# GpSimd waits for the VectorE instruction ahead of it at their shared port: an attention and mixture-of-experts kernel with its order found anew

## The chip, the cores and the metric

The kernel runs on one core of a Trainium2 chip. The metric is the device time of one execution in microseconds. Before the change the median of three runs is 1009.34 us (1007.29 to 1016.77).

## The reference, cut to what matters

Eight batches of 12 heads, 448 tokens, head size 64. Queries and keys are normalised, attention is computed, and its output (3584 tokens of 768) goes through a mixture of experts in which each token uses the one expert of eight that its logits choose.

```python
q_n, k_n = rmsnorm(q, g_q), rmsnorm(k, g_k)
scores = q_n @ k_n.T / sqrt(64)
attn = exp(scores - max) / (sum + 1e-9)
x = (attn @ v) as [3584, 768]
e = argmax(x @ w_gate); gate = softmax(x @ w_gate)[e]
out = gate * sigmoid((x @ w_output_gate)[e]) * (relu(x @ w1[e]) @ w2[e])
```

## The kernel before, in words

The attention part works on 48 head pairs, numbered 0 to 47 (six to a batch). A pair's steps are small operations named `step.pair`, such as `vl.17`. `sq` and `ms` give the mean squares; `n` and `qg` normalise (L419, L424); `hi`, `hj` write the float16 half of queries and keys and `lo`, `lp` the rest (L436); two transposing DMAs `Th`, `Tl` turn them. `M0` to `M3` are score products, of which `x0` to `x3` take the row maxima on VectorE (L456); `NT`, `nt` (L469) turn these; `S0` to `S3` are the scores with the maxima taken off; `e` and `f` are the exponentials as float32 and float16, `p0` to `p3` their difference (L509, on GpSimd or VectorE); `vh`, `vl` split the values in the same way (L515, L519); `A0` to `A3`, `A6` multiply by the values. For the pairs that the string `WHOLE` marks, block 0 isn't split: `Aw` (L535) multiplies it in float32, 16 matrix products, in place of `f0`, `p0` and `A0`. `av1`, `av2`, `av` divide (L553, L556, L562), `tr`, `th`, `lg`, `la` give the router's logits.

After each batch a chain `r0` to `r7` of small VectorE steps picks experts and slots (`r6.e1` to `r6.first_expert` also the first two experts, L763 to L772), and four indirect DMAs `z0` to `z3` from GpSimd (L740) write the slot table. The expert stage then gathers tokens (`xg`, L1006, indirect DMA from GpSimd), splits them (`xh` on ScalarE, `xl` on VectorE, L1053), turns them by DMA (`xt`), splits the weights (`wh` on ScalarE, `wl` on VectorE, L982) and multiplies (`g1`, L1085 to L1087, and `g2`); `sc` scatters rows out (L1100). Only its first steps belong to the order below; the rest of it is in code order.

What order the engines' instructions have is written out by hand in tables: `ENGINES` gives each movable step two engines, `SECOND` picks one by pair, and `RANK` and `ONCE` give each step its place. `Order.run` sorts all steps by place, and the loop in `moe` issues them; each engine takes its own in that order, and waits only for its data and buffers. Each step also carries a mark, `port`, from this table, which nothing before the change reads:

```python
PORT = {
    DVE: ("hi", "hj", "n", "qg", "lo", "lp", "vh", "vl"),
    POOL: ("mh", "n", "qg", "lo", "lp", "p0", "p1", "p2", "p3"),
}
```

The steps `x`, `ms`, `av`, `p` on VectorE read PSUM or one tile and aren't in it; nor are `xl`, `wl` and the chain `r`.

Of the kernel before, what the change touches and what calls it, by code (L numbers as in the profile page):

```python
# [75 lines left out]
    "p0": "100000101110100011110011110001010111101100000110",  # L76
    "p1": "000000000001001001100001101001000000100000000101",
    "p2": "101010000000001011110001000100000000100101010000",
    "p3": "000001011000000100000000000001000001100000010000",
    "lo": "001011111100110100100100000010000000100000001011",  # L80
    "lp": "000011010000101000100100011011010110110101100010",
    "hi": "000000000000000000000000000000000000000000010001",
    "hj": "000000000010000000000000010000001000000010000000",
# [1392 lines left out]
```

## Time and profile before

| what | value |
|---|---|
| median of three runs | 1009.34 us |
| the profiled execution, its own time | 1007.91 us |
| its span, first to last instruction | 1006.1 us |
| mean granted clock of TensorE in it | 0.979 |
| busy in the span: TensorE, VectorE, ScalarE, GpSimd | 91%, 65%, 58%, 46% |

The span is cut by what the core does: attention from 0 to about 506 us, the expert stage from there. Shares over the whole span mix the two, so the rows below are by stretch. In the rows PE is TensorE, DVE VectorE, ACT ScalarE, POOL GpSimd; a name such as `vl<-vf,vh` is output and inputs with buffer numbers left out.

### The profile page before, as it was taken

The page shows a single profiled execution, that of the slowest core. Times are in us where ns is not written, and L with a number is a line of the kernel's source. Part 1 is how long each engine was busy: PE and PEld are TensorE (multiplying, and loading weights), DVE is VectorE, ACT ScalarE, POOL GpSimd, SP SyncE. Part 2 cuts the span into 40 slices and gives each one's busy share as a digit, 9 for nine tenths or more (in the row PEclk, how much of TensorE's full clock was granted, in tenths as well). Part 3 has the DMA queues.
Part 4 walks back from the last instruction along what each step waited for, and adds up shares of the span by engine and source line. Part 5 has one row for each costly group of instructions (what it writes and reads, how often), then busy time and mean ns, then how long its engine had stood idle before and what let it go on. Part 6 is the DMA issues. An engine that isn't in the chain of part 4 may idle for free. (4 is left out here: it accounts for less than half of the span.)

```text
span 1006.1 us, 28072 instructions
## 1 busy us (share of the span) xinstructions
PE 919.1 (91%) x12072; PEld 645.1 (64%) x12072; DVE 658.7 (65%) x1072; ACT 581.9 (58%) x913; POOL 466.0 (46%) x355
## 2 busy tenths in 40 slices
...
GB/s 228 164 177 159 124 208 132 156 114 192 134 163 119 198 169 134 94 108 105 174 237 161 151 262 251 189 108 160 179 119 238 73 209 202 113 225 207 74 2 46
DMA packets 182541, 157.36 MB, mean 156 GB/s; under 512 B 152449, under 2 KB 160263, under 8 KB 176269
## 3 DMA queue, kind: packets, MB, share of 16 engines
...
HBM read 96.73 MB, written 22.59 MB: 119 GB/s over the span
## 5 line engine op out<-in xcount | busy, mean ns | idle before, releaser
L509 POOL TENSOR_TENSOR pl<-p,ph 128x896 f16<-128x896 f32 (+1 forms) x111 | 181.6, 1646 | 54.6 <-PE psa L548 23.0
L456 DVE TENSOR_REDUCE Z<-psM 128x2 f16<-128x896 f32 (+1 forms) x192 | 180.8, 967 | 15.4 <-PE psM L451 11.3
L478 PE MATMUL pss<-ss 64*128 64x448 f16 (+1 forms) x1152 | 146.6, 359 | 10.3 <-DVE Z L456 3.7
L504 ACT ACTIVATE ph<-pss 128x896 f16<-128x896 f32 (+1 forms) x144 | 113.6, 797 | 36.4 <-PE pss L484 27.9
L1085 PE MATMUL g1e<-xTe,w0he 128*128 128x384 f16 x384 | 126.0, 328 | 9.0 <-DMA xTe<-x16e 5.4
L1100 POOL DMA_INDIRECT out<-oe,tie x24 | 25.6, 1068 | 230.4 <-DVE oe L1122 201.5
L1086 PE MATMUL g1e<-xTe,w0he 128*128 128x384 f16 x384 | 125.9, 328 | 0.0
L1087 PE MATMUL g1e<-xTe,w0le 128*128 128x384 f16 x384 | 125.8, 328 | 0.0
L548 PE MATMUL psa<-vh,ph 128*128 128x65 f16 (+1 forms) x1152 | 110.9, 198 | 2.7 <-issue 2.7
L545 PE MATMUL psa<-vl,ph 128*128 128x64 f16 (+1 forms) x1152 | 109.9, 194 | 1.8 <-issue 1.5
L548 PE MATMUL psa<-vh,pl 128*128 128x65 f16 (+1 forms) x1152 | 110.1, 196 | 1.3 <-issue 1.3
L548 PEld LDWEIGHTS <-ph 128*128 128x128 f16 (+1 forms) x1152 | 94.5, 102 | 11.9 <-issue 8.7
L496 ACT ACTIVATE p<-pss 128x896 f32<-128x896 f32 (+1 forms) x120 | 94.9, 798 | 12.2 <-PE pss L484 9.8
L545 PEld LDWEIGHTS <-ph 128*128 128x128 f16 (+1 forms) x1152 | 95.1, 103 | 2.6 <-issue 2.4
L548 PEld LDWEIGHTS <-pl 128*128 128x128 f16 (+1 forms) x1152 | 95.1, 101 | 1.1 <-issue 1.0
L451 PE MATMUL psM<-ss 64*128 64x448 f16 (+1 forms) x384 | 68.9, 375 | 27.2 <-DMA ss<-X 18.5
L1085 PEld LDWEIGHTS <-w0he 128*128 128x128 f16 x624 | 61.5, 99 | 37.2 <-issue 10.0
L484 PEld LDWEIGHTS <-sel 64*128 64x128 f16 (+1 forms) x1536 | 61.8, 99 | 35.5 <-issue 4.5
L478 PEld LDWEIGHTS <-ss 64*128 64x128 f16 (+1 forms) x1152 | 53.3, 98 | 47.7 <-issue 21.4
L1086 PEld LDWEIGHTS <-w0he 128*128 128x128 f16 x624 | 61.6, 99 | 28.6 <-issue 5.1
L1087 PEld LDWEIGHTS <-w0le 128*128 128x128 f16 x624 | 61.6, 99 | 28.3 <-issue 3.7
L982 DVE SCALAR_TENSOR_TENSOR w0le<-wste,w0he 128x1024 f16<-128x1024 f32 x48 | 59.8, 1255 | 27.2 <-ACT w0he L980 27.2
...
## 6 DMA issues: line engine op xcount, KB each, us to landing
...
ss<-X SPq DMA_TRANSPOSE x96
...
tab<-val,slot POOLq DMA_INDIRECT x32
xge<-xs,tie POOLq DMA_INDIRECT x24
```

The source lines that it names most:

```text
L451: T.matmul(o, lhsT=side(0, 0, h, c, n), rhs=side(0, 1, h, 0, S), start=True, stop=True)
L456: V.tensor_reduce(out=o, in_=m, op=ALU.max, axis=AX.X, negate=True)
L478: T.matmul(o[h], lhsT=side(wk, 1, h, 128 * u, n), rhs=side(wq, 0, h, 0, S), start=k == 0, stop=False)
L484: T.matmul(o[h][:, a : a + m], lhsT=self.sel[r, 3 * h + c, 0:n], rhs=st["nt"][r, q], start=False, stop=c == 3)
L496: A.activation(out=t, in_=st[f"S{u}"], func=AF.Exp)
L504: A.activation(out=st[f"ph{u}"], in_=st[f"S{u}"], func=AF.Exp)
L509: return (V if eng == DVE else Pl).tensor_tensor(out=st[f"pl{u}"], in0=st[f"e{u}"], in1=st[f"ph{u}"], op=ALU.subtract)
L545: T.matmul(out[:, 0:D], lhsT=st[f"ph{u}"][:, k, q], rhs=vl[:, jv, :], start=False, stop=False, skip_group_check=True)
L548: T.matmul(out, lhsT=p, rhs=vh[:, jv, :], start=u == j == w == 0, stop=u == 3 and w == 2, skip_group_check=True)
L1085: nc.tensor.matmul(o, lhsT=wh[:, sl], rhs=xT[:, 0, k, 0:n], start=k == 0, stop=False)
L1086: nc.tensor.matmul(o, lhsT=wh[:, sl], rhs=xT[:, 1, k, 0:n], start=False, stop=False)
L1087: nc.tensor.matmul(o, lhsT=wl[:, sl], rhs=xT[:, 0, k, 0:n], start=False, stop=k == KD - 1)
```

## The change

The loop that issues the steps remembers the last VectorE step that is marked `port`. A later GpSimd step that is marked, or that is an indirect DMA (it has a transfer time `xfer`), is made to wait for it; `follow` adds that dependency.

```diff
-WHOLE = "111111111010101010101110111100101010101010100110"
+WHOLE = "111111111010101010101110111100101010101010101111"
...
-                add("xh" + x, ACT, 800, [f"xg{m}.{c}"], lambda q=q, c=c: q["T"][c][0](), [("x16", ["xt" + x])])
-                add("xl" + x, DVE, 860, ["xh" + x], lambda q=q, c=c: q["T"][c][1]())
+                add("xh" + x, ACT, 800, [f"xg{m}.{c}"] + [f"o0.{2 * NCB - 1}"] * (m == 2), lambda q=q, c=c: q["T"][c][0](), [("x16", ["xt" + x])])
+                add("xl" + x, DVE, 860, ["xh" + x] + [f"o1.{2 * NCB - 1}"] * (m == 2), lambda q=q, c=c: q["T"][c][1]())
...
+        held = None
         for o in self.order.run():
-            o["fn"]()
+            ins = o["fn"]()
+            if o["eng"] == DVE and o["port"]:
+                held = ins
+            elif o["eng"] == POOL and None not in (held, ins) and (o["port"] or o["xfer"]):
+                self.follow(ins, [held], "port")
```

All of `SECOND`, `RANK` and `ONCE` is replaced. One line of each of two tables:

```diff
-    "th": "000000000100101010000001000001000000010110010011",
+    "th": "110000001010100000100011010100000001111011000011",
...
-k.edges 0 k.gd 5 k.blank 6 k.cst 7 s00.mean 13 s00.guess 14 s00.sm 17 s00.r 18 k.g 21 s01.mean 22 s01.guess 23 s01.sm 26 s01.r 27 k.flat 28 k.sel 34
+k.edges 0 k.cst 4 k.gd 5 s00.mean 12 s00.guess 13 s00.sm 16 s00.r 17 k.g 20 s01.mean 21 s01.guess 22 s01.sm 25 s01.r 28 k.sel 29 s02.mean 55
```

Pairs 44 and 47 become whole (two more `Aw`, two fewer `f0`, `p0`, `A0`). By step, the number that VectorE does goes from 12 to 18 of `th`, 8 to 13 of `p3`, 14 to 16 of `n`, 21 to 24 of `qg`, 2 to 5 of `vh`; and down from 11 to 9 of `p1`, 6 to 3 of `hi` and `hj` together, 37 to 36 of `lo` and `lp` together. Of `nt` VectorE does 12 where it did 17, ScalarE the rest.

What the waits look like, on GpSimd's queue around the table writes of batch 1 (`slot1`), first before the change. A name's first number is the pair, as in `qkt24` or `pl17_3` (`p3.17`); the bracket names the semaphores that an instruction waits for, those of VectorE as DVE.

```order
L740 DMA tab_85<-val_81,slot1_3580 30720x2
L436 TENSOR_TENSOR X1_119<-qkt22_2299,X1_119 128x8x64 [waits DMAHW6_49]
L419 TENSOR_TENSOR qkt26_3251<-qkt26_3251,y40_3482 128x896 [waits DMAHW4_49]
L509 TENSOR_TENSOR pl16_1_4231<-p3216_1_3831,ph16_1_3837 128x896
L740 DMA tab_85<-val_81,slot1_3580 30720x2
L424 TENSOR_TENSOR qkt24_2638<-qkt24_2638,g_74 128x448 [waits Pool_49]
L509 TENSOR_TENSOR pl17_3_4352<-p3217_3_4217,ph17_3_4254 128x448 [waits PE_49,Activation_49]
L436 TENSOR_TENSOR X1_119<-qkt22_2299,X1_119 128x8x64 [waits Activation_49]
```

And the same place of the changed kernel:

```order
L509 TENSOR_TENSOR pl18_3_4526<-p3218_3_4293,ph18_3_4287 128x448 [waits DVE_49,PE_49,Pool_49]
L740 DMA tab_85<-val_81,slot1_3609 30720x2 [waits DMASW2_49,DMASW3_49,DMASW1_49,DMASW0_49]
L424 TENSOR_TENSOR qkt29_3884<-qkt29_3884,g_74 128x448 [waits Pool_49]
L509 TENSOR_TENSOR pl18_1_4599<-p3218_1_4470,ph18_1_4462 128x896 [waits Activation_49]
L509 TENSOR_TENSOR pl19_1_4654<-p3219_1_4499,ph19_1_4523 128x896 [waits PE_49,Activation_49]
L740 DMA tab_85<-val_81,slot1_3609 30720x2
L740 DMA tab_85<-val_81,slot1_3609 30720x2 [waits DVE_49]
L740 DMA tab_85<-val_81,slot1_3609 30720x2
```

Before, no row of the eight names VectorE; now two do, and rows without the name follow a wait that already covers them. Over all of GpSimd's queue, of the rows of L419, L424, L436, L509, L740, L1006 and L1100, 73 name VectorE's semaphore before and 108 after.

The second place is the handover to the expert stage, GpSimd's queue from the table writes of batch 6 (`slot6`) to the gathers for the first expert (`xge0`). Before:

```order
L740 DMA tab_85<-val_81,slot6_10310 30720x2 x3
L509 TENSOR_TENSOR pl43_1_10535<-p3243_1_10302,ph43_1_10282 128x896 [waits Activation_49]
L509 TENSOR_TENSOR pf44_0_10396<-p3244_0_10407,pf44_0_10396 128x896 [waits Activation_49]
L509 TENSOR_TENSOR pl44_1_10671<-p3244_1_10507,ph44_1_10482 128x896 [waits PE_49,Activation_49]
L509 TENSOR_TENSOR pl44_2_10723<-p3244_2_10604,ph44_2_10583 128x896 [waits Activation_49]
L509 TENSOR_TENSOR pl44_3_10772<-p3244_3_10721,ph44_3_10700 128x448 [waits Activation_49]
L1006 DMA xge0_10767<-xs_84,tie0_10766 128x768 [waits DMAHW5_49,DMAHW6_49,DMAHW4_49,DMAHW7_49,DMAHW1_49,DMAHW0_49]
```

Now:

```order
L740 DMA tab_85<-val_81,slot6_10329 30720x2 x3
L509 TENSOR_TENSOR pl44_1_10691<-p3244_1_10567,ph44_1_10541 128x896 [waits PE_49,Activation_49]
L509 TENSOR_TENSOR pl44_3_10745<-p3244_3_10713,ph44_3_10742 128x448 [waits PE_49,Activation_49]
L509 TENSOR_TENSOR pl45_3_10781<-p3245_3_10689,ph45_3_10693 128x448 [waits PE_49,Pool_49]
L509 TENSOR_TENSOR pl45_1_10804<-p3245_1_10783,ph45_1_10762 128x896 [waits DVE_49,Activation_49]
L509 TENSOR_TENSOR pl45_2_10890<-p3245_2_10855,ph45_2_10797 128x896 [waits DVE_49,Activation_49]
L1006 DMA xge0_10858<-xs_84,tie0_10857 128x768 [waits DMAHW5_49,DMAHW4_49,DMAHW6_49,DMAHW3_49,DMAHW7_49,DMAHW1_49,DMAHW0_49]
```

Three of the four long differences that stood behind the table writes are gone from there (`p1.43`, `p0.44` and `p2.44`; `p0.44` no longer exists), and others with waits on VectorE stand in their place.

## Rows read from the trace of the kernel before

**Rows 1.** Busy time by stretch: stretch, length, then each engine's busy us and instructions

```profile
0.00:50.00 50.00, 24.64 (x266) 13.83 (x268) 42.78 (x59) 37.88 (x71) 36.28 (x44) 0.93 0.75 197
50.00:350.00 300.00, 282.75 (x5229) 209.90 (x5225) 283.01 (x496) 266.24 (x448) 243.35 (x169) 1.00 0.71 155
350.00:450.00 100.00, 95.11 (x1856) 70.92 (x1857) 84.08 (x162) 77.70 (x127) 82.56 (x58) 1.00 0.53 131
450.00:515.00 65.00, 52.63 (x917) 39.39 (x914) 44.57 (x76) 37.04 (x54) 35.87 (x25) 0.89 0.62 153
515.00:1006.00 491.00, 463.97 (x3813) 311.03 (x3811) 204.30 (x283) 163.01 (x216) 67.96 (x62) 0.98 0.54 159
```

**Rows 2.** TensorE's waits, 50 to 515 us: for whom, total us, times, longest

```profile
PE g1e L1085 <- DMA xTe<-x16e: 5.4, 1, 5.4
...
PE pss L478 <- DVE pl L509: 3.2, 2, 2.9
...
PE psa L548 <- DVE xr L562: 2.5, 2, 2.1
```

**Rows 3.** Groups by line and shape, VectorE, 0 to 505 us: busy, mean ns

```profile
L436 DVE TENSOR_TENSOR X<-qkt,X 128x512 f16<-128x512 f32 x37 | 29.3, 804 | 0.7 <-POOL pl L509 0.5
...
L509 DVE TENSOR_TENSOR pl<-pss,ph 128x896 f16<-128x896 f32 x25 | 27.0, 1085 | 5.8 <-issue 2.7 <-ACT pss L493 1.6 <-POOL X L436 1.1
L519 DVE SCALAR_TENSOR_TENSOR vl<-vf,vh 128x384 f16<-128x384 f32 x30 | 20.9, 698 | 0.1
L519 DVE SCALAR_TENSOR_TENSOR vl<-vf,vh 128x512 f16<-128x512 f32 x18 | 17.2, 957 | 0.0
L419 DVE TENSOR_TENSOR qkt<-qkt,y 128x896 f32<-128x896 f32 x14 | 15.1, 1091 | 0.0
L424 DVE TENSOR_TENSOR qkt<-qkt,g 128x448 f32<-128x448 f32 x21 | 14.4, 688 | 0.1
...
L397 DVE COPY xT<-pstr 128x448 f32<-128x448 f32 x10 | 6.1, 607 | 0.1
...
L509 DVE TENSOR_TENSOR pl<-pss,ph 128x448 f16<-128x448 f32 x8 | 4.9, 615 | 0.4 <-PE psa L548 0.4
L469 DVE TENSOR_SCALAR nt<-psNT 128x128 f16<-128x128 f32 x17 | 4.8, 281 | 0.4 <-PE psNT L461 0.4
```

**Rows 4.** Timeline, 199.5 to 206.9 us, GpSimd and then VectorE: start us, us

```profile
200.00 0.97 POOL L740 DMA_INDIRECT tab<-val,slot  x1 [0.17 <-issue]
200.99 1.15 POOL L424 TENSOR_TENSOR qkt<-qkt,g 128x448 f32<-128x448 f32 x1
202.08 1.04 POOL L509 TENSOR_TENSOR pl<-p,ph 128x448 f16<-128x448 f32 x1
203.07 1.16 POOL L436 TENSOR_TENSOR X<-qkt,X 128x512 f16<-128x512 f32 x1
...
200.60 4.18 DVE L519 SCALAR_TENSOR_TENSOR vl<-vf,vh 128x512 f16<-128x512 f32 x1
```

**Rows 5.** Timeline, 460 to 468 us, GpSimd and then VectorE

```profile
460.63 1.90 POOL L509 TENSOR_TENSOR pl<-p,ph 128x896 f16<-128x896 f32 x1
...
464.32 1.88 POOL L509 TENSOR_TENSOR pl<-p,ph 128x896 f16<-128x896 f32 x1
...
461.00 5.23 DVE L764 SCALAR_TENSOR_TENSOR most<-score,top,cst 128x8 f32<-128x8 f32 x1
...
466.34 0.15 DVE L770 SCALAR_TENSOR_TENSOR score<-most,score 128x8 f32<-128x8 f32 x1
```

**Rows 6.** Timeline, 485 to 508 us, VectorE and then TensorE

```profile
485.54 1.04 DVE L1053 TENSOR_TENSOR x16e<-xge,x16e 128x768 f16<-128x768 f32 x1 [2.20 <-ACT x16e L1050]
...
490.35 0.51 DVE L519 SCALAR_TENSOR_TENSOR vl<-vf,vh 128x384 f16<-128x384 f32 x1
490.78 2.64 DVE L1053 TENSOR_TENSOR x16e<-xge,x16e 128x768 f16<-128x768 f32 x1
...
501.25 0.67 DVE L519 SCALAR_TENSOR_TENSOR vl<-vf,vh 128x512 f16<-128x512 f32 x1
...
485.08 1.82 PE L535 MATMUL psa<-vf,pf 128*128 128x65 f32 x16
```

More of the change, by code (lines that the diff above doesn't have):

```diff
@@ L75 @@
 SECOND = {
[L76 to L83, printed above, removed]
@@ new lines @@
+    "p3": "001001000101001000010010001000100000110100000001",
+    "lo": "000011011000101011000011100110100100001010000011",
+    "lp": "000001101011000011100011001010111000010010000000",
+    "hi": "100000000000000000000000000000000000000000000000",
+    "hj": "000000000000000000000000000000000010000000000001",
+    "vh": "000000000000000000000000000000010000001000000111",
+    "th": "110000001010100000100011010100000001111011000011",
+    "n": "000001101010100110100010000110010000100011000010",
@@ L151 @@
-k.ltri 548 k.tab 588 r0.first 613 r0.mx 617 r0.eq 618 r0.ex 619 r0.eqe 620 r0.em 622 r0.oh 627 r0.zz 628 r0.rank 638 k.xs 639 st.0 641 r0.z 644
-r0.count 645 r0.exps 646 r0.pos 649 r0.sum 650 r0.pr 656 r0.sum1 657 r0.slot 661 r0.den 662 s31.mean 684 s31.guess 686 s31.sm 690 s31.r 694 r0.val 756
-s40.mean 864 r0.z0 869 s40.guess 870 s40.sm 876 s40.r 878 r0.z2 890 r0.z1 896 r1.first 899 r1.mx 901 r1.eq 902 r1.eqe 905 r1.ex 906 r0.z3 907
-r1.em 908 r1.oh 911 r1.zz 912 r1.rank 915 r1.z 918 r1.count 920 r1.exps 921 r1.pos 929 r1.sum 930 r1.pr 931 r1.sum1 933 r1.slot 934 r1.den 935
@@ L155 @@
-r1.val 974 st.1 976 r1.z0 978 r1.z1 986 r1.z2 1021 r1.z3 1053 s41.mean 1062 s41.guess 1063 s41.sm 1070 s41.r 1072 s50.mean 1185 s50.guess 1186
-s50.sm 1193 s50.r 1198 st.2 1234 r2.first 1237 r2.mx 1239 r2.eq 1240 r2.eqe 1245 r2.ex 1246 r2.em 1248 r2.oh 1251 r2.zz 1254 r2.z 1257 r2.exps 1279
-r2.rank 1294 r2.count 1302 r2.pos 1307 r2.sum 1308 r2.pr 1316 r2.sum1 1318 r2.slot 1319 r2.den 1325 r2.val 1326 s51.mean 1346 s51.guess 1348
-r2.z0 1349 s51.sm 1352 s51.r 1354 r2.z1 1377 r2.z3 1390 r2.z2 1400 s60.mean 1548 s60.guess 1549 s60.sm 1556 s60.r 1557 r3.first 1623 r3.mx 1628
@@ L159 @@
-r3.eq 1629 r3.eqe 1631 r3.em 1632 r3.ex 1634 r3.oh 1637 r3.zz 1645 r3.z 1647 r3.rank 1658 r3.count 1664 r3.exps 1669 r3.sum 1671 r3.sum1 1673
-r3.pos 1674 r3.den 1675 s61.mean 1685 s61.guess 1687 r3.pr 1692 s61.sm 1694 s61.r 1695 r3.slot 1698 r3.val 1716 r3.z0 1736 r3.z1 1742 r3.z2 1770
-st.3 1822 r3.z3 1828 s70.mean 1867 s70.guess 1870 s70.sm 1875 s70.r 1876 r4.first 1904 r4.mx 1906 r4.eq 1911 r4.ex 1913 r4.eqe 1915 r4.em 1917
-r4.oh 1918 r4.zz 1919 r4.rank 1942 st.4 1946 r4.z 1947 r4.exps 1950 r4.count 1955 r4.sum 1959 r4.pos 1960 r4.pr 1962 r4.sum1 1963 r4.den 1967
@@ L163 @@
-r4.slot 1968 s71.mean 2021 s71.guess 2026 r4.val 2028 s71.sm 2036 s71.r 2037 r4.z3 2098 r4.z0 2105 st.5 2162 r5.first 2184 r5.mx 2188 r5.eq 2190
-r5.ex 2191 r5.eqe 2193 r5.em 2195 r5.oh 2197 r5.zz 2203 r5.z 2225 r5.exps 2234 r5.rank 2288 r5.count 2292 r5.sum 2295 r5.pos 2296 r5.sum1 2298
-r5.pr 2299 r5.den 2300 r5.slot 2302 r4.z1 2313 r4.z2 2321 r5.val 2350 r5.z0 2369 r5.z1 2377 r5.z3 2383 r5.z2 2392 st.6 2418 r6.first 2439 r6.mx 2442
-r6.eq 2445 r6.eqe 2446 r6.ex 2447 r6.em 2448 r6.oh 2449 r6.zz 2450 r6.rank 2451 r6.z 2454 r6.count 2458 r6.exps 2459 r6.sum 2461 r6.pos 2463
@@ L179 @@
[L179 to L180 removed]
+k.edges 0 k.cst 4 k.gd 5 s00.mean 12 s00.guess 13 s00.sm 16 s00.r 17 k.g 20 s01.mean 21 s01.guess 22 s01.sm 25 s01.r 28 k.sel 29 s02.mean 55
+s02.guess 56 s02.sm 64 k.flat 65 s02.r 68 s10.mean 109 s10.guess 110 s10.sm 115 k.blank 117 s10.r 123 k.wg 183 s11.mean 199 s11.guess 206 s11.sm 213
@@ new lines @@
+s11.r 217 k.tab 308 s20.mean 367 s20.guess 369 s20.sm 373 s20.r 382 s21.mean 410 s21.guess 411 s21.sm 417 s21.r 422 s30.mean 527 s30.guess 537
+s30.sm 545 s30.r 546 r0.first 583 k.ltri 587 r0.mx 590 r0.eq 592 r0.eqe 599 r0.em 600 r0.oh 601 r0.zz 603 r0.z 607 r0.ex 608 r0.exps 647 r0.rank 650
+r0.count 655 s31.mean 656 s31.guess 657 s31.sm 661 r0.pos 662 r0.sum 665 s31.r 666 r0.sum1 668 r0.pr 670 r0.den 671 r0.slot 673 r0.val 725 k.xs 750
+r0.z1 799 st.0 800 r0.z0 810 r0.z3 833 r0.z2 839 s40.mean 857 s40.guess 858 s40.sm 863 s40.r 865 r1.first 901 r1.mx 904 r1.eq 906 r1.eqe 908 r1.em 909
@@ new lines @@
+r1.oh 910 r1.ex 911 r1.zz 912 r1.z 917 r1.rank 935 r1.count 946 r1.exps 949 r1.sum 951 r1.pos 952 r1.sum1 954 r1.pr 956 r1.slot 958 r1.den 959
+r1.val 988 s41.mean 1024 st.1 1029 s41.guess 1030 s41.sm 1041 s41.r 1050 r1.z1 1126 r1.z3 1158 r1.z0 1179 r1.z2 1186 s50.mean 1190 s50.guess 1196
+s50.sm 1201 s50.r 1204 r2.first 1228 r2.mx 1232 r2.eq 1237 r2.eqe 1242 r2.em 1246 r2.oh 1247 r2.ex 1248 r2.zz 1251 r2.z 1268 r2.exps 1273 st.2 1298
+r2.rank 1302 r2.count 1310 r2.pos 1315 r2.sum 1316 r2.pr 1317 r2.sum1 1318 r2.den 1322 r2.slot 1324 r2.val 1329 r2.z2 1336 r2.z1 1344 r2.z3 1348
@@ new lines @@
+s51.mean 1353 s51.guess 1355 s51.sm 1358 s51.r 1361 r2.z0 1438 s60.mean 1534 s60.guess 1556 s60.sm 1562 s60.r 1564 r3.first 1619 r3.mx 1627 r3.eq 1629
+r3.eqe 1631 r3.ex 1633 r3.em 1635 r3.oh 1640 r3.zz 1644 r3.z 1650 st.3 1668 s61.mean 1670 r3.exps 1671 r3.rank 1678 s61.guess 1680 r3.count 1683
+r3.sum 1690 s61.sm 1691 r3.pos 1693 r3.sum1 1695 s61.r 1699 r3.pr 1701 r3.den 1702 r3.slot 1703 r3.val 1709 r3.z2 1747 r3.z1 1766 r3.z3 1775
+s70.mean 1869 s70.guess 1870 s70.sm 1882 s70.r 1884 r4.first 1918 r4.mx 1925 r4.eq 1929 r4.eqe 1931 r4.em 1933 r4.ex 1935 r4.oh 1936 r4.zz 1938
@@ new lines @@
+r4.z 1941 r3.z0 1953 r4.exps 1960 r4.rank 1961 r4.count 1966 r4.sum 1971 r4.pos 1972 r4.sum1 1974 r4.pr 1976 r4.den 1979 r4.slot 1981 r4.val 1999
+s71.mean 2008 s71.guess 2011 r4.z2 2021 s71.sm 2027 s71.r 2029 st.4 2043 r4.z3 2046 r4.z0 2055 r4.z1 2064 r5.first 2182 r5.mx 2186 r5.eq 2189
+r5.eqe 2190 r5.em 2191 r5.ex 2192 r5.oh 2194 r5.zz 2197 r5.z 2208 st.5 2209 r5.exps 2252 r5.rank 2253 r5.count 2261 r5.sum 2265 r5.sum1 2267
+r5.pos 2269 r5.pr 2271 r5.den 2272 r5.val 2276 r5.slot 2277 r5.z1 2360 r5.z2 2366 r5.z0 2371 r5.z3 2388 r6.first 2444 r6.mx 2448 r6.ex 2450 r6.eq 2451
@@ new lines @@
+r6.eqe 2454 r6.em 2460 r6.oh 2463 r6.zz 2464 r6.rank 2466 r6.z 2473 r6.count 2474 r6.exps 2475 r6.sum 2477 r6.e0 2478 r6.pos 2479 r6.pr 2483
+r6.sum1 2485 r6.slot 2488 r6.den 2489 st.6 2490 r6.val 2491 r6.z3 2496 r6.z0 2500 r6.e1 2503 r6.e2 2505 r6.e3 2506 r6.e4 2508 open1 2509 r6.z2 2511
+r6.z1 2517 r6.e5 2529 r6.e6 2542 r6.e7 2543 r6.first_expert 2548 ti0 2560 ld0.0 2562 ti1 2565 units 2571 xg0.0 2573 xg0.1 2579 r6.gap 2585 xg0.2 2586
+xh0.0 2598 xg1.0 2599 xl0.0 2604 wh0.0 2605 xt0.0 2609 xh0.1 2611 xl0.1 2616 xt0.1 2620 ld0.1 2624 xh0.2 2629 xl0.2 2636 wl0.0 2640 xt0.2 2642
@@ new lines @@
+ld0.2 2646 xg1.1 2648 wh0.2 2652 xg1.2 2653 wh0.1 2656 r6.gap1 2659 g1.0 2661 wh0.3 2662 wl0.2 2663 wl0.1 2665 wh0.4 2666 wl0.3 2667 ld0.3 2669
+g1.1 2670 xh1.0 2671 ld0.4 2673 xh1.2 2674 g1.2 2675 wh0.5 2676 hh.1 2677 hl.1 2678 g1.3 2680 wl0.4 2682 wl0.5 2683 hh.3 2685 ld0.5 2686 g1.4 2687
+open2 2688 wh0.6 2690 wh0.9 2691 wl0.6 2692 wh0.7 2693 xl1.0 2694 r7.first 2695 g1.5 2696 wh0.8 2697 hl.3 2698 xt1.0 2699 r7.mx 2700 r7.eq 2701
+wl0.9 2702 wh0.11 2703 wl0.7 2704 g1.6 2705 wh0.10 2706 wl0.11 2707 ld1.0 2708 xh1.1 2709 wl0.10 2710 hh.5 2711 g1.7 2712 r6.bump 2713 r7.eqe 2714
```

32 lines of the change are left out of this document (12 added, 20 removed), and 106 rows, old and new, of the table RANK.

## The prediction

> **What bounds the kernel now.** I read the busy time by stretch first, since the two stages have different limits [rows 1]. From 515 us on nothing on VectorE (204 of 491 us busy) or GpSimd (68) is near full, and TensorE is busy for 464 of 491: the expert stage belongs to TensorE. Its code isn't touched after the first steps, and a GpSimd transfer there that now waits for a marked VectorE step waits for one that ended long ago, since the last one belongs to pair 47. I cost that stage at nothing.
>
> In attention the picture is another. Between 50 and 350 us VectorE is busy for 283.0 of 300 us, TensorE for 282.8, ScalarE for 266.2, GpSimd for 243.4. TensorE's number flatters it: its busy time includes matmuls that overlap one another, so a small gap between two of them hides. VectorE's instructions run nearly one after the other, and 17 us of idle time in 300 is what a queue in fixed order leaves. So VectorE is the tightest engine up to 350 us; behind that it is looser (84.1 of 100, then 44.6 of 65).
>
> Next I asked whether VectorE's busy time is work. The groups by shape say no [rows 3]: the 18 wide `vl` take 957 ns on average, and an undisturbed one takes 0.67 us [rows 6]; the 30 narrow ones 698 against 0.51. The timeline shows what happens in the worst case [rows 4]: at 200.60 a `vl` starts while GpSimd writes the table, GpSimd then runs three two-input instructions back to back until 204.23, and the `vl` ends at 204.78 after 4.18 us, about 0.67 us behind the last of them. It was held 3.5 us, by several instructions in a row and not by one. Behind it TensorE stands 2.9 us for a difference `pl` that VectorE had queued [rows 2].
>
> The Trainium skill, page "SBUF — State Buffer", section "Who interferes with whom", calls this an exclusive lock on one pair of ports, taken by whoever starts first, for VectorE instructions with two SBUF inputs and GpSimd ones that read SBUF. The 4.18 us agree with that.
>
> **The change, part by part.** (1) The waits. GpSimd may no longer start a marked instruction ahead of the marked VectorE step that stands before it. What it can give is the stretch of the marked VectorE steps. Wide `vl`: 18 x (957 - 670) = 5.2 us. Narrow `vl`: 30 x (698 - 510) = 5.6 us. `lo` and `lp` have the shape of the wide `vl`; with its 670 ns, 37 x (804 - 670) = 5.0 us [rows 3, 6]. Together 15.8 us. It isn't all to be had: a VectorE step that comes due while a GpSimd instruction already runs still waits for the rest of that one; what ends is that a second and a third one slip in. The bounds are 0 and 15.8; the one case that I can see whole is wholly of the kind that ends (3.5 us), the shorter ones are mixed, and I take six tenths, 9.5 us.
>
> (2) What the waits cost GpSimd. 35 more of its instructions name VectorE. Behind each stands GpSimd's own queue, and behind that the `A` products that need a `p`. GpSimd has 57 us idle in 300 and 17 in 100 [rows 1], and loses work on balance: fewer `p3`, `n`, `qg`, and two `p0` that are no longer there. A wait costs it up to the length of a marked VectorE step, 0.5 to 1.1 us, but part of that it pays today as a stretched instruction of its own. From below the cost is 0, from above 35 x 0.67 = 23 us; within its idle time it is hidden, and I take 0. If the cover is gone, the third rival below has the price.
>
> (3) Work moved to VectorE [rows 3]: six more copies `th` at 607 ns, 3.6 us; five `p3` at 615, 3.1; two `n` at 1091, 2.2; three `qg` at 688, 2.1; less two `p1` at 1085, 2.2, and five `nt` at 281, 1.4. That is 7.4 us more; three `vh` more, three casts and one `lo` less I set at -1 us together. 6.4 us, all on the engine that I named as the bound. So (1) and (3) make -9.5 + 6.4 = -3.1 us.
>
> (4) The handover, 450 to 515 us. TensorE is busy for 52.6 of 65 us there [rows 1]; its longest wait but the first is 5.4 us at the first expert product, for the turned tokens [rows 2]. The chain that leads there holds two stalls at the same port. The tiny `most` of the chain that names the first expert takes 5.23 us at 461.00, while three long `p` run on GpSimd from 460.63 to 466.20; a like instruction takes 0.15 [rows 5]. And one `xl` takes 2.64 us where its like takes 1.04 [rows 6]. Neither `most` nor `xl` is marked, so no wait protects them; only the order can. It does in part: `p0.44` is gone, three long `p` no longer stand behind the table writes, and the router step of batch 6 comes earlier among the products. From 0 to all of 5.4 + 2.1 us (the second is TensorE's wait for `xr`, which is queued behind `most` [rows 2]): for the tokens I take half, 2.7, and for `most` 2.1, because its three neighbours are spread now.
>
> (5) Two more `Aw`. One takes 1.82 us on TensorE [rows 6]; the 24 short products that go take between nothing and the same. So 0 to 3.6 us for two, of which I count 1.1. In exchange ScalarE and GpSimd each lose two instructions. The two extra conditions on the third gather's split bear on steps that come after the first expert's last products, and cost nothing that I can see.
>
> Sum: -3.1 - 2.7 - 2.1 + 1.1 = -6.8 us. The profiled execution took 1007.9 us, 1.8 more than its span of 1006.1; so 1001.1, and I say 1001. It is 1.4 under the median of the runs, and I don't correct for that.
>
> **The rivals.** *The whole stall comes back.* VectorE recovers all 15.8 us and the handover all 7.5: -15.8 + 6.4 - 7.5 + 1.1 = -15.8, or 992. For it speaks that a plan in which the chip keeps the planned order loses nothing to accidents; against it that ScalarE is at 266 of 300 and becomes the next limit, and that unmarked steps still lose the port.
>
> *The loser changes, the loss stays.* The port is held for as long as before; VectorE no longer waits, but GpSimd waits the same and its `p` come later, while VectorE has 6.4 us more to do. Of the 9.5 us of (1) a GpSimd delay of about 3 is taken off, 6.5; the moved work of 6.4 eats that; the handover gives half of what I counted, 2.4, or nothing: 1005 to 1008. Against it, GpSimd with 243 of 300 us busy isn't quite full and can wait at no cost. The exclusive lock of the Trainium skill (same page and section) speaks for it, since a lock that is held as long as before only changes who waits; no run here shows yet which of the two waits is dearer. That few waits are new (35) belongs here too: if most pairs kept their order anyway, the change is a new draw of the order and little more.
>
> *GpSimd becomes the late engine.* This is the side on which it gets slower. VectorE takes its queue in order, and a marked step may stand there behind a maximum that waits for TensorE, which waits for a `p` of GpSimd; GpSimd now waits in turn for the marked step though the port is free. Half of the 35 new waits on the path at 0.67 us are 12 us, with the 6.4 us of moved work 18, less the 4 that a quarter of the 15.8 would still give back: +14, or 1022. It decides once GpSimd's idle time in a stretch falls below a tenth. The 350 to 450 stretch, with 82.6 of 100 us busy, is where it would show first; against it stands that GpSimd is ahead of its plan, as the early table write shows [rows 4], rather than behind.
>
> **How the numbers follow.** My forecast, 40%, with 995 to 1007 as its own range. The whole stall, 23%. The loss that stays, 23%. GpSimd late, 14%. A change of 1% either way (999 and 1019) is about what a measurement of this kernel can tell from none. All of the second case and four tenths of the first are below 999: 23 + 16 = 39, and I say 0.40. Above 1019 lies most of the last case and a little of the third, 0.16. The rest is 0.44. The range of 8 in 10 leaves out the lower part of the whole stall and the upper part of the late GpSimd: 988 to 1018.
>
> **What would show it right or wrong.** Step 1: the mean of both `vl` groups falls towards 510 and 670 ns and that of `lo`, `lp` towards 670; no VectorE instruction of that kind is over 2 us. If the means stay, the waits sit at other places than the stalls. Step 2: GpSimd's idle time grows ahead of L509 and L436 with VectorE as releaser, while TensorE's waits for `pl` don't. Step 3: VectorE's busy time from 0 to 505 us falls by about 3. Step 4: the first expert product starts before 502 us and the wait for the turned tokens is under 3. The forecast is wrong if attention ends at 506 us or later, or if the difference comes from the stretch behind 515.

## The result, and the profile after

The changed kernel takes 985.96 us (median of 4 runs, 985.31 to 986.8); the kernel before, run beside it, 1010.17 (4 runs). The ratio is 0.9737, 95% interval 0.9707 to 0.9767. Forecast were 1001 us and a range of 988 to 1018: right in direction, three times too small in size, and outside the range. The profiled execution took 986.28 us (span 984.4, clock 0.985).

The same kernel before took 974 us in the first two sets below and 1010 to 1014 in the other two and beside this result, for a cause that no run settles (the second and the third set have the same chip number on record), so ratios are always against the kernel before of the same set, and instants are compared only between measurements in which it took the same time.

Busy time by stretch of the changed kernel, columns as in [rows 1]:

```profile
0.00:50.00 50.00, 25.40 (x274) 14.13 (x275) 42.91 (x61) 36.84 (x69) 33.83 (x43) 0.93 0.82 205
50.00:350.00 300.00, 285.72 (x5312) 211.25 (x5309) 280.08 (x499) 268.13 (x454) 228.35 (x165) 1.00 0.73 156
350.00:450.00 100.00, 97.25 (x1848) 72.16 (x1840) 88.19 (x174) 78.42 (x128) 79.19 (x58) 1.00 0.60 117
450.00:515.00 65.00, 60.99 (x943) 44.48 (x943) 39.68 (x81) 40.67 (x55) 27.47 (x21) 0.97 0.71 200
515.00:984.00 469.00, 445.87 (x3696) 299.31 (x3694) 194.85 (x269) 153.90 (x206) 68.12 (x62) 0.98 0.55 161
```

Between 50 and 350 us little is different from [rows 1]: VectorE 280 against 283, TensorE 286 against 283. The stretch that changed is 450 to 515: TensorE busy for 61.0 us against 52.6, at a granted clock of 0.97 against 0.89.

TensorE's waits of the changed kernel, 50 to 515 us (for whom, total us, times, longest):

```profile
PE psa L548 <- issue: 4.7, 10, 1.2
PE psM L451 <- ACT p L496: 2.0, 3, 1.4
...
PE pss L478 <- DVE pl L509: 0.8, 2, 0.4
```

Of the three waits in [rows 2] the 5.4 us for the turned tokens and the 2.5 us for `xr` are gone, and that for `pl` fell from 3.2 to 0.8.

VectorE's groups by line and shape of the changed kernel, 0 to 505 us (busy, mean ns), which answer to [rows 3]:

```profile
L436 DVE TENSOR_TENSOR X<-qkt,X 128x512 f16<-128x512 f32 x36 | 24.8, 711 | 0.0
L519 DVE SCALAR_TENSOR_TENSOR vl<-vf,vh 128x384 f16<-128x384 f32 x32 | 19.7, 619 | 0.0
L419 DVE TENSOR_TENSOR qkt<-qkt,y 128x896 f32<-128x896 f32 x16 | 18.6, 1161 | 0.0
L424 DVE TENSOR_TENSOR qkt<-qkt,g 128x448 f32<-128x448 f32 x24 | 16.5, 700 | 0.1
L519 DVE SCALAR_TENSOR_TENSOR vl<-vf,vh 128x512 f16<-128x512 f32 x16 | 13.1, 819 | 0.0
```

The narrow `vl` fell from 698 to 619 ns, the wide one from 957 to 819, `lo` and `lp` from 804 to 711. Beside the undisturbed lengths of [rows 3, 6] 32 x 109, 16 x 149 and 36 x 41 ns are left, 7.4 us where 15.8 stood: 8.4 are won. VectorE's whole busy time from 0 to 505 us fell from 451.5 to 442.6.

To see where the whole gain sits I read five instants off each profiled execution and took the stretches between them: the end of the 42nd of 48 attention outputs `xr` (L562); the first second-layer product `g2` of the first expert; the first `g1` of the second expert (L1085); the first `g1` of that expert's tail (`g1e0t`); the last product of all. The second stretch, from 42nd output to first `g2`, is called the handover here.

| us | to the 42nd output | handover | first expert's `g2` | second expert | rest | sum |
|---|---|---|---|---|---|---|
| before | 445.8 | 91.4 | 23.4 | 28.0 | 410.1 | 998.7 |
| changed | 441.7 | 80.1 | 23.4 | 23.4 | 408.3 | 976.9 |
| difference | -4.1 | -11.3 | 0 | -4.6 | -1.8 | -21.8 |

Half of the gain is the handover and a fifth the second expert, which I had at nothing. The handover's own busy time, before and then changed, columns as in [rows 1]:

```profile
445.80:537.20 91.40, 79.03 (x1147) 56.33 (x1144) 63.02 (x107) 49.95 (x70) 37.86 (x26) 0.93 0.65 173
441.70:521.80 80.10, 75.18 (x1103) 53.99 (x1100) 52.54 (x109) 49.08 (x68) 35.21 (x26) 0.98 0.68 190
```

TensorE's idle time there falls from 12.4 to 4.9 us, by 7.5, and its busy time by 3.8, while the granted clock rises from 0.93 to 0.98.

### The profile page after: what moved, and what is told of

Same layout as the page of the kernel before. It is cut to its first block, busy times and chain, and to the rows that moved or that the text cites. A ratio compares the mean times of both kernels' runs of the same rounds, so it can differ in the third digit from the quotient of the medians.

```text
span 984.4 us, 28049 instructions
## 1 busy us (share of the span) xinstructions
PE 915.2 (93%) x12056; PEld 641.3 (65%) x12056; DVE 645.7 (66%) x1080; ACT 578.0 (59%) x910; POOL 437.0 (44%) x346
## 5 line engine op out<-in xcount | busy, mean ns | idle before, releaser
L509 POOL TENSOR_TENSOR pl<-p,ph 128x896 f16<-128x896 f32 (+1 forms) x108 | 174.4, 1624 | 56.2 <-ACT ph L504 10.4
L1100 POOL DMA_INDIRECT out<-oe,tie x24 | 25.8, 1076 | 241.6 <-DVE oe L1122 213.4
L1085 PE MATMUL g1e<-xTe,w0he 128*128 128x384 f16 x384 | 125.2, 326 | 0.3 <-issue 0.3
L496 ACT ACTIVATE p<-pss 128x896 f32<-128x896 f32 (+1 forms) x115 | 92.6, 810 | 19.7 <-PE pss L484 15.9
L548 PEld LDWEIGHTS <-ph 128*128 128x128 f16 (+1 forms) x1152 | 93.3, 101 | 12.3 <-issue 9.0
L545 PEld LDWEIGHTS <-ph 128*128 128x128 f16 (+1 forms) x1152 | 94.0, 102 | 3.3 <-issue 3.1
L1085 PEld LDWEIGHTS <-w0he 128*128 128x128 f16 x624 | 61.8, 100 | 31.0 <-issue 7.1
L436 POOL TENSOR_TENSOR X<-qkt,X 128x512 f16<-128x512 f32 x60 | 68.8, 1160 | 28.5 <-ACT ph L504 5.4
L478 PEld LDWEIGHTS <-ss 64*128 64x128 f16 (+1 forms) x1152 | 51.9, 98 | 42.4 <-issue 14.2
```

The costliest lines, as they stand in the source:

```text
L436: return (V if eng == DVE else Pl).tensor_tensor(out=X[:, 1, :, :, d], in0=x, in1=X[:, 0, :, :, d], op=ALU.subtract)
L478: T.matmul(o[h], lhsT=side(wk, 1, h, 128 * u, n), rhs=side(wq, 0, h, 0, S), start=k == 0, stop=False)
L496: A.activation(out=t, in_=st[f"S{u}"], func=AF.Exp)
L509: return (V if eng == DVE else Pl).tensor_tensor(out=st[f"pl{u}"], in0=st[f"e{u}"], in1=st[f"ph{u}"], op=ALU.subtract)
L545: T.matmul(out[:, 0:D], lhsT=st[f"ph{u}"][:, k, q], rhs=vl[:, jv, :], start=False, stop=False, skip_group_check=True)
L548: T.matmul(out, lhsT=p, rhs=vh[:, jv, :], start=u == j == w == 0, stop=u == 3 and w == 2, skip_group_check=True)
```

## The experiments

Four sets were run; in each the kernel before was timed again. The stretches are those of the table above.

**First set (the kernel before: 973.71 us): the order and the waits apart.** My theory was that the waits give VectorE its lost time back, the rival that the new order alone does it. e1 is the changed kernel without its wait:

```diff
-            elif o["eng"] == POOL and None not in (held, ins) and (o["port"] or o["xfer"]):
-                self.follow(ins, [held], "port")
```

> The changed kernel with the waits taken out: the new order alone, same instructions, 33 fewer of GpSimd's rows that name VectorE. Theory W (the waits carry the gain, since they stop GpSimd from starting ahead of a marked VectorE step): the wide vl goes back towards 950 ns from 819, and the time to 1000 or more of the 986. Theory O (the new order carries it, above all at the handover to the expert stage between 450 and 515 us, where the old one lost TensorE some 15 us): 984 to 990, with the first expert product still near 495 us, even if single VectorE steps are stretched again. A mixture would lie at 993 or so.

Measured: 1000.43 us, ratio 1.0297 (1.0218 to 1.0377). e2 is the opposite, the order of before with the waits:

> The kernel before with the waits alone, in the old order, with the old choice of engines and of whole pairs: 49 more of GpSimd's rows name VectorE. Theory W: 990 to 998, since most of the 15.8 us of stretch of marked VectorE steps goes. Theory O: 1003 to 1010, the stretch goes but the handover keeps its 5.4 us wait for the turned tokens and the 5 us stall of the unmarked step at 461 us. If GpSimd becomes late by the waits, 1012 or more.

Measured: 972.44 us, ratio 0.9998 (0.9961 to 1.0035). Neither half gives anything: the order alone loses 3%, the waits alone nothing. In e3 and e4 the waits cover more VectorE steps, those that I had found unprotected, in the old and in the new order:

```diff
-            if o["eng"] == DVE and o["port"]:
+            if o["eng"] == DVE and (o["port"] or o["name"].startswith(("xl", "wl0", "r6.e"))):
```

> The kernel before with the waits, and with the unmarked VectorE steps of the handover (xl, the first expert's wl, and the chain r6.e) marked as well, so that GpSimd waits for these too. If what the old order lost at the handover was the port (5.23 us for a step of 0.15, 2.64 for one of 1.04), this recovers 5 to 10 us against the same kernel without these marks. If it was the order of the work, it comes out within 3 us of that kernel.

> The changed kernel with the same extra marks. In its trace the unmarked steps are hardly stretched any more, so both theories expect no change: 984 to 988. Slower (990 or more) if waiting for the weights' split holds up GpSimd's last differences or its gathers.

Measured: e3 964.15 us, 0.9933 (0.9902 to 0.9964); e4 953.32, 0.9836 (0.9761 to 0.9911). So in the old order the three extra kinds of mark are worth something that the marks of the change are not; e4 can't be told from the changed kernel (0.980 in r1 below).

| us, first set | to the 42nd output | handover | second expert | rest |
|---|---|---|---|---|
| e1, new order, no waits | 485.9 | 74.3 | 23.4 | 387.3 |
| e2, old order, waits | 434.5 | 87.4 | 30.8 | 388.3 |
| e3, old order, more waits | 433.9 | 77.6 | 30.1 | 387.9 |
| e4, new order, more waits | 434.0 | 73.9 | 23.4 | 387.6 |

The table splits the question in two. To the 42nd output the waits decide, and only in the new order: e4 is 51.9 us ahead of e1 (and r1 of the second set, the changed kernel itself, 51.5). In the handover and at the second expert the order decides: e1 has both gains with no wait at all, and loses only before them.

VectorE's groups in e1, 0 to 505 us, show how it loses:

```profile
L436 DVE TENSOR_TENSOR X<-qkt,X 128x512 f16<-128x512 f32 x36 | 38.3, 1087 | 0.0
L519 DVE SCALAR_TENSOR_TENSOR vl<-vf,vh 128x384 f16<-128x384 f32 x28 | 29.3, 1052 | 0.0
...
L519 DVE SCALAR_TENSOR_TENSOR vl<-vf,vh 128x512 f16<-128x512 f32 x16 | 16.3, 1019 | 0.0
```

The same steps that take 711, 619 and 819 ns in the changed kernel (728, 621 and 792 in r1) take 1087, 1052 and 1019. Against the changed kernel that is 13.5 + 12.1 + 3.2 = 29 us on an engine with little idle time. TensorE's waits of e1, 50 to 450 us, are for what stands behind them in VectorE's queue, the row maximum `Z` above all (and for `vl` itself); in r1 no wait for `Z` comes to more than 0.5 us:

```profile
PE psM L451 <- DVE Z L456: 8.9, 6, 3.1
PE pss L478 <- DVE Z L456: 8.5, 9, 3.0
PE psa L545 <- DVE vl L519: 5.0, 5, 1.7
```

And one row for each of four traces tells how the `vl` of 50 to 500 us fare (instructions, then ns of the shortest, the median and the longest). The kernel before, in its first trace and then in r2 of the second set, where it took as long as beside e2:

```profile
L519 DVE SCALAR_TENSOR_TENSOR vl<-vf,vh x46: 505/620/4185, 54.3 to 490.4; 128x384 f16<-128x384 f32 x29, 128x512 f16<-128x512 f32 x17
...
L519 DVE SCALAR_TENSOR_TENSOR vl<-vf,vh x47: 507/675/2240, 54.2 to 493.4; 128x384 f16<-128x384 f32 x29, 128x512 f16<-128x512 f32 x18
```

e2, the old order with the waits, and who waited for these `vl` (us, times):

```profile
L519 DVE SCALAR_TENSOR_TENSOR vl<-vf,vh x47: 506/689/2205, 53.8 to 492.3; 128x384 f16<-128x384 f32 x29, 128x512 f16<-128x512 f32 x18
...
  POOL tab L740: 9.0, 7
```

The changed kernel:

```profile
L519 DVE SCALAR_TENSOR_TENSOR vl<-vf,vh x46: 543/613/1356, 58.0 to 484.1; 128x384 f16<-128x384 f32 x30, 128x512 f16<-128x512 f32 x16
```

In e2 the waits do take hold (GpSimd stands 9.0 us for `vl` ahead of table writes), and still one `vl` takes 2.2 us and the median is no shorter: beside r2 the waits changed next to nothing. A wait binds only GpSimd instructions that stand behind a VectorE step in the order. The traces, with each instruction's place in its kernel's order, show how many do. Counted is each meeting, over 50 ns long, of a VectorE step of L419, L424, L436 or L519 with GpSimd arithmetic of L419, L424, L436 or L509:

| meetings | GpSimd's instruction stands ahead | behind |
|---|---|---|
| r2, old order, no waits | 63 | 25 |
| e2, old order, waits | 58 | 2 |
| e1, new order, no waits | 73 | 27 |
| r1, new order, waits | 40 | 0 |

So in the old order the waits end nearly all that they can, and the larger part stays, which no wait binds (the `vl` of 2.2 us is held by an instruction that stands ahead). In the new order, 33 of the 73 meetings with instructions ahead go with the waits as well, and no `vl` of the changed kernel is over 1.36 us. Why these go is not shown: that the order was laid out for engines that keep in step is my reading, and I made no run with that alone altered.

**Second set (the kernel before: 973.84 us): which waits, and both kernels again.** f1 has only the waits of GpSimd's arithmetic, f2 only those of its indirect DMAs; r1 is the changed kernel, r2 that of before.

```diff
-            elif o["eng"] == POOL and None not in (held, ins) and (o["port"] or o["xfer"]):
+            elif o["eng"] == POOL and None not in (held, ins) and o["port"]:
```

> [...] Ratio 0.970 to 0.977 if the first measurement holds anywhere; a ratio of 0.98 or more would say that part of the first gain was that chip's. The new order with the extra marks gave 0.984 (0.976 to 0.991) on the chip of the first four runs: if the extra marks do nothing, this one gives the same there.

> The kernel before as it is, for a trace on the same chip: ratio 1.000. The question to its trace is where its VectorE instructions are stretched and how that differs from the first trace. Theory S (attention's length follows VectorE's stretch one for one): stretch and the time of the last attention product move together, 20 to 30 us of stretch.

> The new order with the waits on GpSimd's marked arithmetic alone: its indirect DMAs don't wait. If the port conflict is one between reading instructions only, these waits carry all of the gain: within 4 us of the changed kernel. If the writing of descriptors is held up by and holds up VectorE too, or if DMAs that start early let the arithmetic slip, 5 us or more are lost.

> The new order with the waits on GpSimd's indirect DMAs alone, 36 of them in the ordered part. Nearly all of the stretch without any wait (52.7 us of VectorE in attention) should stay: within 8 us of the new order without waits, that is a ratio to the kernel before of 1.02 to 1.03. If the DMAs' waits act as brakes that keep GpSimd from running ahead for long stretches, it recovers half of the loss.

Measured: r1 954.97 us, 0.9802 (0.9746 to 0.9858); r2 973.68, 0.9988 (0.9957 to 1.002); f1 951.17, 0.9754 (0.971 to 0.9799); f2 995.09, 1.0213 (1.0166 to 1.0261). To the 42nd output f1 takes 433.1 us and r1 434.4, f2 473.2. The waits of the arithmetic do all; those of the DMAs win 13 of e1's 52 us back by themselves, and add nothing to the others. I had expected 0.970 to 0.977 for r1; 0.980 is above that, but its interval and that of the first ratio overlap, so whether the gain is smaller here stays open.

| us, second set | to the 42nd output | handover | second expert | rest |
|---|---|---|---|---|
| r2, before | 433.4 | 89.8 | 30.7 | 388.3 |
| r1, changed | 434.4 | 73.6 | 23.4 | 388.8 |

Here the changed kernel costs and gains nothing in the body, and everything comes from the two stages behind it: -16.2 and -7.3 us. Between r2 and the first trace of the same kernel, the theory that attention's length follows VectorE's stretch one for one fails: `lo` and `lp` take 819 ns on average in r2 and 804 in the first trace, wide `vl` 835 and 957, narrow ones 726 and 698, while the body takes 433 and 446 us, and the rest behind the second expert 388 and 410. The cause of the two gains can be read in r2. TensorE's waits there, 430 to 585 us:

```profile
PE psM L451 <- DVE Z L456: 6.2, 1, 6.2
PE pss L478 <- ACT ph L504: 5.4, 1, 5.4
PE g1e L1085 <- DVE oe L1122: 4.5, 1, 4.5
```

The same view of r1:

```profile
PE pbe0t L1160 <- ACT yTe0t L1155: 1.9, 1, 1.9
PE psk L727 <- DVE oh L698: 0.7, 1, 0.7
```

Three waits, 16.1 us, that r1 hasn't. The first: timeline of r2, 448 to 459 us, GpSimd and then VectorE (start, us):

```profile
448.25 1.89 POOL L509 TENSOR_TENSOR pl<-p,ph 128x896 f16<-128x896 f32 x1
450.09 1.89 POOL L509 TENSOR_TENSOR pf<-p,pf 128x896 f16<-128x896 f32 x1
451.93 3.71 POOL L509 TENSOR_TENSOR pl<-p,ph 128x896 f16<-128x896 f32 x2
...
448.60 7.06 DVE L764 SCALAR_TENSOR_TENSOR most<-score,top,cst 128x8 f32<-128x8 f32 x1
455.70 0.16 DVE L765 TENSOR_REDUCE first<-most 128x1 f32<-128x8 f32 x1
```

The step `most`, on eight numbers per partition, takes 7.06 us, until the last of four long `p` is done. This is the 5.23 us of [rows 5] again, and longer; `Z` stands behind it, and TensorE for `Z`. What the clock does meanwhile is shown by the stretch from 450 to 460 us in r2:

```profile
450.00:460.00 10.00, 3.78 (x64) 2.50 (x61) 9.41 (x7) 1.09 (x2) 5.63 (x4) 0.68 0.02 4
```

and in r1:

```profile
450.00:460.00 10.00, 10.00 (x194) 7.84 (x190) 6.89 (x15) 7.77 (x12) 7.70 (x7) 1.00 0.38 125
```

TensorE is busy for 3.8 of those 10 us, and the granted clock averages 0.68: for a part of them it is at the lower of its two levels, 1.2 GHz. In r1 `most` takes 0.84 us at most (and in e1, with no wait, 0.83):

```profile
L764 DVE SCALAR_TENSOR_TENSOR most<-score,top,cst x2: 228/536/843, 448.2 to 454.6; 128x8 f32<-128x8 f32 x2
```

e3 marks `most`, `xl` and `wl0` in the old order and gives the price of the three together: `most` takes 1.62 us, TensorE's longest waits for `Z` and for `ph` fall from e2's 6.1 and 3.4 us to 0.8 and to none, and the handover falls from 87.4 to 77.6 us.

```profile
449.07 1.62 DVE L764 SCALAR_TENSOR_TENSOR most<-score,top,cst 128x8 f32<-128x8 f32 x1
...
PE psM L451 <- DVE Z L456: 1.0, 2, 0.8
```

What lies between 77.6 us and the changed kernel's 73.6 was not taken apart.

The second wait is the path to the turned tokens; r2, 470 to 490 us, ScalarE and then VectorE:

```profile
475.19 0.92 ACT L1050 ACTIVATE x16e<-xge 128x768 f16<-128x768 f32 x1
...
486.06 0.84 ACT L1050 ACTIVATE x16e<-xge 128x768 f16<-128x768 f32 x1 [9.15 <-DMA xTe<-x16e]
...
471.95 3.76 DVE L1053 TENSOR_TENSOR x16e<-xge,x16e 128x768 f16<-128x768 f32 x1 [1.32 <-ACT x16e L1050]
```

An `xl` takes 3.76 us where 0.95 is its mean in the changed kernel's first gathers, and ScalarE stands 9.15 us because the third of these splits needs one of two buffers back (`x16`), while `ph` for the attention stands behind it. The third wait has its place at the second expert: r2, 533 to 566 us, ScalarE and then VectorE:

```profile
554.54 0.84 ACT L1050 ACTIVATE x16e0t<-xge0t 128x768 f16<-128x768 f32 x1 [7.15 <-DMA xge0t<-xs,tie0t]
555.29 0.56 ACT L1120 ACTIVATE oe<-g2e,tie 128x384 f32<-128x384 f32 x1
...
562.35 0.60 DVE L1122 TENSOR_SCALAR oe<-g2e,tie 128x384 f32<-128x384 f32 x1
```

ScalarE waits 7.15 us for the third gather, with the first expert's last outputs `oe` queued behind it; TensorE needs the bank that `oe` frees. In the changed kernel the two added conditions put that split behind `oe`.

**Third set (the kernel before: 1012.0 us): repairs in the old order.** g1 puts the two outputs ahead of the third gather's split; g2 adds e3's waits and a third `x16` buffer; g3 is f1 with that buffer; g4 is the changed kernel with pairs 44 and 47 cut up as before.

```diff
+        at["o0.1"], at["o1.1"] = at["sc.3"] + 0.3, at["sc.3"] + 0.6
...
-                x16[c] = self.kp.tile([128, 2, DM], F16, tag="x16", name=f"x16{nm}_{c}")
+                x16[c] = self.kp.tile([128, 2, DM], F16, tag="x16", bufs=3, name=f"x16{nm}_{c}")
...
-WHOLE = "111111111010101010101110111100101010101010101111"
+WHOLE = "111111111010101010101110111100101010101010100110"
...
```

> The kernel before, without waits, with one edit: the last output steps o0.1 and o1.1 of the first expert stand ahead of the split of the third gather on ScalarE and VectorE, as the changed kernel's two extra conditions demand. In the old trace of the second chip ScalarE waits 7.2 us for that gather with the output step behind it, and TensorE waits 4.5 us for the PSUM tile at the second expert's products, with a clock drop behind it. If these two lines are what the changed kernel gains between 547 and 577 us, this comes out 5 to 8 us faster than the kernel before (ratio 0.992 to 0.995). If the third gather itself is what is late, no change.

> The old order with three repairs: the waits with the extra marks (0.993 alone), the outputs ahead of the third gather's split (5 to 8 us), and three buffers in place of two for the split tokens, since in the old order ScalarE stood 9.2 us for the transposing DMA of the first one and TensorE 5.4 us. If the changed kernel's gain is these three local stalls, their removal in the old order gives all of it: 9.5 to 12 + 5 to 8 + 3 to 5 us, that is 950 to 956 where the kernel before is at 973.7, ratio 0.975 to 0.982. If the new order gains by its whole body (engines, pairs, places), this stays above 0.985.

> The new order with waits on GpSimd's marked arithmetic alone (ratio 0.975 where the changed kernel was at 0.980) and three buffers for the split tokens. The changed kernel's ScalarE still has 1.7 us of idle time for that buffer, so 0 to 2 us less: 0.973 to 0.976. A candidate to beat both kernels.

> The changed kernel with pairs 44 and 47 split again: f0, p0 and A0 put in beside e0 and ahead of the other products, in place of Aw. If Aw costs TensorE what its 1.8 us say, the split is 0 to 2 us faster; if what counts is the work taken from GpSimd, ScalarE and VectorE at the handover, the split is 1 to 5 us slower. Ratio to the kernel before 0.978 to 0.986.

Measured: g1 1010.54 us, 1.0023 (0.9982 to 1.0065); g2 992.18, 0.9809 (0.9773 to 0.9845); g3 985.2, 0.9749 (0.971 to 0.9788); g4 990.65, 0.9799 (0.9757 to 0.9841). g1 failed: the second expert still takes 31.1 us. The wait only moved, as TensorE's waits, 515 to 620 us, show (one line of code more, so lines are one higher):

```profile
PE g1e L1086 <- DVE he1l L1096: 5.3, 1, 5.3
```

and ScalarE's timeline, 560 to 590 us:

```profile
585.09 1.06 ACT L981 ACTIVATE w1he<-wste 128x1024 f16<-128x1024 f32 x1 [6.57 <-DMA wste<-w]
```

Now the weights come late: ScalarE waits 6.57 us for a load (`wste`) whose split stands ahead of `he1h`, which `he1l` needs (the float16 halves of the second expert's hidden values). On SyncE's queue the transposes of the third gather (`xTe0t`, L1063) stand ahead of two weight loads in the old order and behind them in the new one:

```order
L1063 DMA_TRANSPOSE xTe0t<-x16e0t_11978 128x12x16
L956 DMA wste_4_11986<-w 128x2048
L1063 DMA_TRANSPOSE xTe0t<-x16e0t_11973 128x12x128
L956 DMA wste_5_11995<-w 128x2048
```

So the loads wait for transposes, these for splits, and these for the gather; moving the outputs alone can't help. In g2 the handover takes 79.1 us against 92.8 in g1, mostly what e3 had shown already; what the third buffer adds there can't be told apart. g3 and g4 settle nothing more: a third buffer is worth nothing to the new order, and the two whole pairs may be worth up to 5 us of handover (85.4 in g4; 80.3 in g3, 80.1 in the first profile of the changed kernel), but the intervals overlap, and g3 differs in the waits and the buffer too.

**Fourth set (the kernel before: 1013.85 us): the second expert's cause.** The open question was whether the third gather's split, queued on three engines ahead of weight work, holds the second expert. h1 takes the old order without waits and g1's line, and moves that split and its transposes behind the weight work; h2 is g2 with it. h3 is f1 again, h4 the changed kernel again.

```diff
+        at.update({f"{x}2.{c}": at["o1.1"] + 6 + c + k / 4 for c in range(2) for k, x in enumerate(("xh", "xl", "xt"))})
```

> The kernel before, without waits, with the outputs o0.1 and o1.1 and all weight splits and weight loads ahead of the third gather's split and its transposing DMAs on ScalarE, VectorE and SyncE. If TensorE's 4.5 to 5.3 us at the second expert's products come from that gather standing ahead of the weights in three queues, this is 4 to 7 us faster than the kernel before: ratio 0.993 to 0.996, and the wait at the second expert is gone. If not, 0.998 to 1.002.

> The old order with this, the waits with the extra marks, and three buffers for the split tokens. The three repairs gave 0.981 (0.977 to 0.985). If the new order gains by these places alone, this reaches it: 0.973 to 0.977, within 3 us of the changed kernel in this call. If part of the gain is the new order's body, it stays 5 us or more behind.

> The changed kernel with the waits on GpSimd's marked arithmetic alone, again, beside the changed kernel in the same call. It was at 0.975 against 0.980 before. If the transfers' waits cost something, it is 2 to 5 us under the changed kernel; if that was scatter, within 1.5 us.

> The changed kernel again, as the yardstick of this call: ratio to the kernel before 0.972 to 0.982, from 0.974 and 0.980 so far.

Measured: h1 1006.63 us, 0.9936 (0.9904 to 0.9968); h2 991.83, 0.9793 (0.9747 to 0.9838); h3 988.22, 0.9763 (0.9728 to 0.9798); h4 988.3, 0.9755 (0.972 to 0.979). The second expert takes 24.1 us in h1, 24.0 in h2. TensorE's waits of h1, 515 to 620 us (two lines more):

```profile
PE pbe0t L1162 <- ACT yTe0t L1157: 1.7, 1, 1.7
...
PE g1e L1087 <- DVE he1l L1097: 0.6, 1, 0.6
```

The 5.3 us of g1 are 0.6 here. g1 and h1 differ in the place of the third split and its transposes alone, so that cause is shown. f1's lead of 3.8 us over the changed kernel didn't come back in h3, so I take it for scatter, and no version I ran beats the changed kernel by more than that. With four local repairs the old order (h2) comes to 0.9793 against 0.9755 of h4; to the 42nd output it is 4.2 us behind (447.1 against 442.9), elsewhere within 2 us. The intervals overlap, so what remains may be nothing.

## Why the prediction was wrong

**Terms (1) to (3), the body, -3.1 us: right in size, wrong as a sum.** The table gives -4.1 in the first profiles, +1.0 in r1 against r2, and -7.1 in h4 against h1, whose edits lie behind the body. The 9.5 us to be won by the waits measured 8.4. But I priced the waits and the new order as two terms that add. They don't: waits alone 0, order alone +52 us by the 42nd output, both together -7 to +1. The single stall that I took as the model, 4.18 us at 200.60 [rows 4], misled. Of the three instructions that held it two stand behind it in the order, and a wait would end those; but of all 91 meetings in that trace, counted as above, 63 are with instructions that stand ahead. So I read as overtaking what for the larger part was the order itself. (That `vl` ended 0.55 us, not 0.67, behind the last of the three.) My condition "if the means stay, the waits sit at other places than the stalls" describes e2: `lo` and `lp` are at 816 ns there, against 819 in r2.

The Trainium skill, page "SBUF — State Buffer", section "Who interferes with whom", says that whoever issues first gets the shared pair of ports for the whole instruction, and that "Issue order, not op shape, decides who blocks." The second sentence agrees with e1 and r1, whose same shapes take 1087 and 728 ns. By the first alone a step would be held for at most the rest of one GpSimd instruction, 1.89 us in r2's rows. That agrees with 24 of the 27 cases that the last section counts in r2, and not with `most`, 7.06 us through four.

**Term (2), waits at no cost to GpSimd: agrees.** Ahead of its long differences GpSimd stood 35.1 us before, mostly for TensorE, and stands 26.0 now, for VectorE first; ahead of `X` (L436) the time grew from 10.9 to 28.5, and TensorE's wait for `pl` still fell. GpSimd's groups, 0 to 490 us, before and then changed:

```profile
L509 POOL TENSOR_TENSOR pl<-p,ph 128x896 f16<-128x896 f32 x69 | 134.2, 1950 | 35.1 <-PE psa L548 19.4 <-ACT p L496 5.4 <-PE psNT L461 3.7
L509 POOL TENSOR_TENSOR pl<-p,ph 128x896 f16<-128x896 f32 x72 | 135.6, 1891 | 26.0 <-DVE vl L519 4.8 <-DVE rc L556 3.4 <-DVE qkt L424 3.4
```

**Term (4), the handover, -2.7 and -2.1: mis-sized.** These are the steps that failed first: "for the tokens I take half, 2.7, and for `most` 2.1". The handover measured -11.3 us in the first profiles and -16.2 in r1 against r2. I had found both stalls and their cause, and e3 bears it out: waits on `most`, `xl` and `wl0` alone are worth 9.8 us of the old order's handover. But I took only 4.8 of the 7.5 us that the rows showed, and that upper end was too low as well. In the first profiles TensorE's idle time in the handover fell by just that 7.5; the other 3.8 us are busy time, at a granted clock of 0.93 before and 0.98 now, which I had put at nothing. That row was in my hand: 0.89 in [rows 1] for 450 to 515 us, 0.97 now. I took it for something given, though stalls of TensorE stand in that stretch. Of r1's 16.2 us against r2, in the same way, 12.7 are idle time and 3.5 busy time; there ScalarE also stands 9.15 us for a buffer, a wait that the first trace doesn't show.

**Term (5), two more `Aw`, +1.1: not separated.** g4 and the others differ by less than their intervals; if anything the whole pairs gain.

**The expert stage, "I cost that stage at nothing": failed.** It gave -4.6 us at the second expert (-7.3 in r1 against r2). The very sentence is "the two extra conditions on the third gather's split bear on steps that come after the first expert's last products, and cost nothing that I can see". I looked for what they cost and not for what stood in the queue before: ScalarE's outputs behind a split that waits for a gather, and SyncE's weight loads behind transposes that wait for the split.

**The rivals.** The result lies nearest to "the whole stall comes back" (992), but not for its reason: 8.4 of the 15.8 us came back, and the rest came from behind. "The change is a new draw of the order and little more" is true of both later stages and false of the body, where the new order without its waits is 3% slower than before. "GpSimd becomes the late engine" didn't come about. (The sums of "the loser changes" and of this rival leave out the 1.1 us of term (5): with it they give 1006 to 1009, and 1023.) Of my signs, no `vl` is over 2 us, as said; VectorE's busy time from 0 to 505 us fell by 9.0 instead of 3; the first expert product starts at 494.9 us instead of 506.1, as said; that the difference would not come from behind 515 us was half wrong, since about 6 of the 22 us do.
